# Building the kv operand of a Toeplitz convolution on VectorE in 32-bit words instead of on GpSimd

## The chip, the cores and the metric

The kernel runs on one core of a Trainium2 chip. The metric is the device time of one execution in microseconds (us); of five runs of the kernel before, the median is 862.05 us (856.38 to 877.54). All detail comes from one profiled execution of the same program.

## What is computed

Two independent heads, laid side by side in the output (2048 positions, 640 channels each):

```python
# A: gated long convolution, one filter of length S = 2048 per channel
k_shift = sum(k_pad[:, t:t + S, :] * shift_k[:, ks - 1 - t] for t in range(4))
kv = k_shift * v
y  = causal_convolution(kv, ssm_k) + kv * ssm_D      # the reference does it by FFT
a  = q * y
# B: softmax attention, 32 heads of 20 channels
q, k, v = split(x @ wqkv)
b = (softmax(q @ k.T * 20 ** -0.5) @ v) @ wo
out = concat([a, b], axis=-1)
```

All inputs and the output are bf16.

## The kernel before

**The attention sets the order of the work.** It is cut into 2,048 *units*: the scores of one head for 512 queries and 128 keys, 128 x 512 fp32, one PSUM bank each. Four units (four heads, placed in the four row strips of TensorE) share a key block. For each unit TensorE computes the scores (`S_task`, L629), an engine takes the exponential, and TensorE multiplies the probabilities with V (`PV_task`, L749), summing 16 key blocks in bank 6. Banks 0 to 2 and 3 to 5 are two halves of three units that alternate. ScalarE takes the exponential of all three units of a half in one instruction (`EXP_task`, L671, 128 x 1536), or of two (128 x 1024) while VectorE takes the third, which the text calls a *vector unit*: L691 brings it from PSUM to SBUF as 16-bit integers, and a chain of six short operations for one or two such units at a time (L721 to L731) makes the exponential by a polynomial on bit patterns. `want_vec` (L1191) decides for each half whether there is a vector unit; it asks for less than `VQ` microseconds of work queued for VectorE, and for a key block below the limits `KBV`, `KBW`.

**The convolution** is a sum of matrix products with Toeplitz blocks. A first stage (`kv_iter`, L555) makes kv on VectorE out of the shifted k, the filter taps and v (132 steps, the multiplications at L558) and writes it to a scratch tensor in DRAM in reversed order. After it, `conv_setup` (L925) starts the second stage, which runs through the rest of the kernel in 40 tasks of 16 channels. Its buffers:

- `KVr`, 128 x 64 x 80 bf16: kv of 80 channels, loaded by four DMAs (`kvr_load`, L940) every five tasks, eight times in all.
- `KVX[i]`, two buffers of 128 x 1024 bf16: for one task, kv of 16 channels, copied out of `KVr` in the order that the matmuls read. Per channel 64 columns: four groups (32-row shifts) of 16 time blocks. `kvx_build` (L950) makes it; the build of task t+2 is put in line after the last matmul of task t (L988).
- `HK`: four buffers with the Toeplitz rows of four channels each, loaded by DMA (`hk_load`).

`conv_task` (L964) issues 128 matmuls a task (L982), each with its own 128 x 128 weight load and only 26 to 32 moving columns, which it reads from `KVX` as two runs of 13 to 16 adjacent columns. They go to bank 7. Three VectorE operations (L999, L1000, L1002) bring a task's result to SBUF. `A_iter` (L1013) multiplies with q and writes the output for 160 channels at a time, 64 small steps (L1020).

In the kernel before, `kvx_build` makes two steps of 128 x 512 bf16 for GpSimd (L957): a copy whose source runs with a step of 320 elements (640 bytes) in its innermost dimension. These are GpSimd's only work in the second stage, apart from one memset (L933).

**The order on every engine is written out at build time** by a planner (L1280 to L1385). It keeps a clock for each engine, gives each operation a cost, and at each step takes for TensorE the next piece that is ready: scores, products with V, projections (L473), a few matmuls of a convolution task, or, where nothing else fits, a *filler*: a matmul of zeros (L376, `fill`, L1268) that keeps TensorE active. A filler is put in if the active time planned in the last 3.4 us is under `ZTH` and the next scores are more than `ZSL` us away (L1378); it is two matmuls if they are more than 0.45 us away. VectorE's order comes from `dve_run` (L1165): of the candidates that could start now, the one with the lowest priority number. GpSimd's came from `pool_run` (L1151). The planner holds VectorE operations that are marked as ones that share a memory port with GpSimd (`two`) back until 0.3 us before a planned GpSimd copy ends (L1133), or, if they start inside it, takes them to end 0.31 us after it (L182). Landing times of DMAs are planned as well, with 2.5 us added to the planned transfer (L193). The plan is an estimate: on the chip, engines run their lists in order and wait on semaphores.

Constants of the planner that the change touches: `KV0`, `KVPACE` (from when and at how many steps per us `kv_iter` counts as late, L1120), `APACE` (the same for `A_iter`), `VQ`, `CONVE` (how many units before the last the convolution should be done, L1204), `ZSL`, `AGE` (when an old chain of VectorE rises in priority, L1135), `LONE` (when a chain with one vector unit is closed, L1194).

Of the kernel before, what the change touches and what calls it, by code (L numbers as in the profile page):

```python
# [6 lines left out]
ALU = mybir.AluOpType  # L7
FP32 = mybir.dt.float32
BF16 = mybir.dt.bfloat16
I32, I16, U16 = mybir.dt.int32, mybir.dt.int16, mybir.dt.uint16  # L10

S = 2048
D = 640
# [16 lines left out]
NPAIR = 48  # L30
OBS = 99
NXB = 3
KBV, KBW, LONE = 13, 12, 16
CQ = 0.026
KV0, KVPACE, APACE, VQ, CONVE, ZTH, AGE, WAIT3 = 25.0, 0.8, 0.25, 4.5, 60, 2.3, 32, 0.4
TAND = 0.287
DOV, DDEP, SWITCH = 0.085, 0.03, 0.105


EXP_C = (0.07826797, 0.30457564)  # L40
DMAX = 2.0
ZSL, ZLO = 0.45, 1.8
LAT = {"pe": 0.12, "act": 0.1, "dve": 0.06, "pool": 0.1}


# [4 lines left out]
def sub(base, dims, offset=0, p0=0, pn=None):  # L50

    b = base if pn is None else base[p0:p0 + pn]
    pd = list(b.ap[0])
    return bass.AP(tensor=b.tensor, offset=b.offset + offset, ap=[pd] + [list(d) for d in dims])
# [218 lines left out]
def build_kernel(nc, A_q, A_k, A_v, A_shift_k, A_ssm_k, A_ssm_D, B_x, B_wqkv, B_wo, out):  # L273
# [3 lines left out]
    with ExitStack() as es:  # L277
        E = es.enter_context
        P = Prog(nc, E)
# [27 lines left out]
        HK_E, KVR_E, KVX_E, Y_E, AST_E = 4 * HKW, 64 * 80, 16 * 64, 16 * 160, 160  # L307
# [10 lines left out]
        def carve(n):  # L318
            a = R[:, pos[0]:pos[0] + n]
            pos[0] += n  # L320
            return a
# [6 lines left out]
        xst = [carve(4 * D).rearrange("p (t d) -> p t d", t=4) for _ in range(4)]  # L328
        pos[0] = 0
        HK = [carve(HK_E) for _ in range(NHK)]  # L330
        KVr = carve(KVR_E).rearrange("p (j c) -> p j c", j=64)
        KVX = [carve(KVX_E) for _ in range(2)]
        Y = [carve(Y_E).rearrange("p (t c) -> p t c", t=16) for _ in range(2)]
        Aq = [carve(AST_E) for _ in range(NAQ)]
# [34 lines left out]
             reads=[b_ident], writes=[b_ident])  # L369
# [26 lines left out]
        for i in range(4):  # L396
            P.dma("sp", xst[0][:, i, :], x2[i * 128:(i + 1) * 128, :], DS("x0%d" % i), writes=[b_x0[i]])
        P.op("sp", lambda e: e.dma_start(xst[1], ap(x2, [[D, 128], [128 * D, 4], [1, D]], 512 * D)),
             writes=[b_xst[1]], dsem=DS("x1"), extra=b_x0[1].w, kb=640, c=0.45)
# [13 lines left out]
        def work(prio, steps, after=None):  # L413
            if not live[0]:
                for fn, rd, wr, c, two in steps:
                    P.op("dve", fn, reads=rd, writes=wr, c=c, two=two)
                if after:
                    after()
                return None
            w = Work(prio, steps, after)  # L420
            works.append(w)
            return w
# [497 lines left out]
        cv = {}  # L920
# [19 lines left out]
        def kvr_load(b):  # L940
            P.dmas("sp", [(KVr[32 * a:32 * a + 32, 16 * a:64, :],
                           ap(kvr_d, [[D, 32], [32 * D, 64 - 16 * a], [1, 80]], 80 * b)) for a in range(4)],
                   d_kvr, reads=b_kvd, writes=[cv["KVr"]], slow=2)
# [5 lines left out]

        def kvx_build(t):  # L950
            i = t % 2
            kx = cv["KVX"][i]
            steps = []
            for z in range(2):
                dst = sub(KVX[i], [[64, 8], [16, 4], [1, 16]], 512 * z)
                src = sub(KVr, [[1, 8], [80, 4], [320, 16]], t % 5 * 16 + 8 * z)
                steps.append((lambda e, dst=dst, src=src: e.tensor_copy(dst, src), [cv["KVr"]], [kx], 1.3, False))  # L957
            pworks.append(Work(0, steps, lambda: kvr_load(t // 5 + 1) if t % 5 == 4 and t < 39 else None))

        def conv_reads(bt):  # L960
            rd = [cv["HK"][4 * bt % NHK], cv["HK"][(4 * bt + 1) % NHK], cv["KVX"][bt % 2]]
# [2 lines left out]
        def conv_task(bt):  # L964

            B, j = divmod(bt, 10)
            i = bt % 2
            for u in range(4):
                qd = bt * 4 + u
                sl = qd % NHK  # L970
                rd = [cv["HK"][sl], cv["KVX"][i]]
                for x in range(4):
                    for k in range(8):
                        d, r1 = divmod(k, 2)
                        n = 16 - d
                        last = x == 3 and k == 7
                        lhsT = HK[sl][:, x * HKW + 128 * d - 32 * r1 + 32:x * HKW + 128 * d - 32 * r1 + 160]
                        rhs = sub(KVX[i], [[32, 2], [1, n]], (4 * u + x) * 64 + r1 * 16)
                        o = sub(bank[MISC], [[256, 2], [1, n]], (4 * u + x) * 16 + d)
                        st = u + x + k == 0  # L980
                        yield (CQ, rd if x + k == 0 else [])
                        P.op("pe", lambda e, o=o, lhsT=lhsT, rhs=rhs, st=st, k=k: e.matmul(  # L982
                            o, lhsT, rhs, start=st, stop=k == 7, skip_group_check=True),
                            reads=rd, writes=[bkb[MISC]], tok=last, c=CQ, st=2 * n / 2400)
                        if last:
                            if qd + NHK < 160:
                                hk_load(qd + NHK)
                            if u == 3 and bt + 2 < 40:  # L988
                                kvx_build(bt + 2)
            M, Yb = bank[MISC], Y[B % 2]  # L990

            def after():
                conv_done[0] += 1
                if j == 9:
                    micro.append([A_iter(B), None])
                    mark[:] = [micro_n[0], P.T["pe"]]

            y, bz = cv["Y"][B % 2], cv["Z"]
            work(0.8, [(lambda e: e.tensor_copy(ZS[64:128], sub(M, [[1, 16], [16, 16]], 256, 0, 64)), [bkb[MISC]], [bz[0]], 0.425, False),  # L999
                       (lambda e: e.tensor_copy(ZS[0:64, 16:256], sub(M, [[1, 15], [16, 16]], 256, 64, 64)),  # L1000
                        [bkb[MISC]], [bz[1]], 0.41, False),
                       (lambda e: e.tensor_tensor(sub(Yb, [[160, 16], [1, 16]], 16 * j), sub(M, [[1, 16], [16, 16]]),  # L1002
                                                  ZS.rearrange("p (t x) -> p t x", t=16), ALU.add),
                        [bkb[MISC]] + bz, [y], 0.425, False)], after)

        conv_done = [0]
        pworks = []

        def A_load(B, tp):
            i = tp % NAQ  # L1010
# [137 lines left out]
                            r = max(r, busy - 0.3)  # L1148
                        yield max(T, r), 1.5 if micro_late(now) else 3, m

        def pool_run(until):  # L1151
            while P.T["pool"] <= until:
                for w in pworks:
                    st = w.steps[w.i]
                    if P.ready("pool", st[1], st[2], me=st) <= until:
                        P.op("pool", st[0], reads=st[1], writes=st[2], c=st[3], me=st)
                        w.i += 1
                        if w.i == len(w.steps):
                            pworks.remove(w)
                            w.after()  # L1160
                        break
                else:
                    return

        def dve_run(until):  # L1165
            while True:
                c = list(dve_cands(until))
# [113 lines left out]
        while nu[0] < NU or npv[0] < NB - 1 or conv_b < 40 or conv or side or pend or tail[0] < 2:  # L1281
            now = P.T["pe"]
            k = nu[0]
            bnow = k // 4
            dve_run(now)
            pool_run(now)
            P.flush(now)
            if not added and all(("X", t) in done for t in range(NKB)):
                added.append(1)
# [48 lines left out]
            if not side:  # L1338
                x = pick(bnow + 6, slack, now, bnow)
# [29 lines left out]
            if not side:  # L1369
                x = pick(NB, slack, now, bnow)  # L1370
# [9 lines left out]
            P.T["pe"] = now + 0.03  # L1380
        while micro or works or P.late:
            dve_run(P.T["pe"])
            pool_run(P.T["pe"])
            P.flush(P.T["pe"])
            P.T["pe"] += 0.1  # L1385
        live[0] = False
# [75 lines left out]
```

## Time and profile before

| | |
|---|---|
| median of five runs | 862.05 us |
| the profiled execution's own time | 864.96 us |
| its span, first to last instruction | 863.2 us |
| TensorE busy | 834.5 us, 11,659 matmuls |
| ScalarE busy | 823.7 us, 738 instructions |
| VectorE busy | 770.6 us, 1,582 instructions |
| GpSimd busy | 102.4 us, 95 instructions, 80 of them the copies of L957 |
| granted TensorE clock, mean | 0.973 of full speed |

An engine's busy time counts its instructions; waiting and issuing do not count. For TensorE it is of little use by itself, since matmuls overlap and 435 of them are fillers. A line such as "L957 POOL COPY R<-R 128x512 bf16 x80 | 90.2, 1127 | ..." reads: source line, engine (PE is TensorE, PEld its weight loads, DVE VectorE, ACT ScalarE, POOL GpSimd, SP the queue that issues most DMAs), operation, output and input tile (`R` is the memory that holds `HK`, `KVr`, `KVX`, `Y` and the probabilities), shape, count; then busy us in all and mean ns of one; then the engine's idle time just before them and what ended it.

### The profile page before, as it was taken

The page shows a single profiled execution, that of the slowest core. Times are in us where ns is not written, and L with a number is a line of the kernel's source. Part 1 is how long each engine was busy: PE and PEld are TensorE (multiplying, and loading weights), DVE is VectorE, ACT ScalarE, POOL GpSimd, SP SyncE. Part 2 cuts the span into 40 slices and gives each one's busy share as a digit, 9 for nine tenths or more (in the row PEclk, how much of TensorE's full clock was granted, in tenths as well). Part 3 has the DMA queues.
Part 4 walks back from the last instruction along what each step waited for, and adds up shares of the span by engine and source line. Part 5 has one row for each costly group of instructions (what it writes and reads, how often), then busy time and mean ns, then how long its engine had stood idle before and what let it go on. Part 6 is the DMA issues. An engine that isn't in the chain of part 4 may idle for free.

```text
span 863.2 us, 27035 instructions
## 1 busy us (share of the span) xinstructions
PE 834.5 (97%) x11659; PEld 357.6 (41%) x11659; DVE 770.6 (89%) x1582; ACT 823.7 (95%) x738; POOL 102.4 (12%) x95
## 2 busy tenths in 40 slices
PE   9999999999999999999999999999999999999998
PEld 5432332222245344454434534453443444444432
DVE  4557799998689899999999999999998999999994
ACT  6799999999789999999999999999998999999996
POOL 3000000003011121212111111211111111111100
PEclk9999999999579899999999999999998999999999
DMA  9704432219158776968876696987759469977812
GB/s 274 226 26 147 155 98 92 93 56 151 36 148 158 163 192 171 182 159 194 160 173 149 173 197 149 199 172 174 174 150 181 116 176 197 179 160 160 191 33 60
DMA packets 172994, 130.35 MB, mean 151 GB/s; under 512 B 76977, under 2 KB 170155, under 8 KB 172875
## 3 DMA queue, kind: packets, MB, share of 16 engines
q1 hardware_dynamic: 170683, 125.51, 62.7%
q0 software_dynamic: 736, 2.75, 0.9%
q8 instruction: 92, 1.51, 0.8%
q10 hardware_dynamic: 1456, 0.37, 0.2%
q14 instruction: 27, 0.22, 0.1%
HBM read 120.58 MB, written 10.61 MB: 152 GB/s over the span
## 4 chain that ended last, share of the span: by engine, by line
DVE 39%; ACT 35%; PE 24%; issue 1%; DVEq 0%
ACT R L671 35%; DVE XV L691 8%; PE PS L629 7%; PE PS L982 4%; DVE XF L728 4%; DVE XF L731 4%; PE PS L749 4%; DVE R L721 3%; PE PS L376 3%; DVE R L558 3%; PE PS L473 3%; DVE XF L726 3%; DVE XF L727 2%; DVE XF L729 2%; DVE ZS L1000 1%
## 5 line engine op out<-in xcount | busy, mean ns | idle before, releaser
L671 ACT ACTIVATE R<-PS 128x1024 bf16<-128x1024 f32 (+1 forms) x730 | 819.1, 1357 | 25.4 <-PE PS L629 25.0
L629 PE MATMUL PS<-QT,KT 20*128 20x512 bf16 x2048 | 289.1, 392 | 15.1 <-ACT R L671 5.4
L982 PE MATMUL PS<-R 128*128 128x32 bf16 (+3 forms) x5120 | 214.7, 177 | 0.5 <-DVE R L1002 0.3
L982 PEld LDWEIGHTS PS<-R 128*128 128x128 bf16 x5120 | 164.5, 96 | 105.2 <-issue 96.6
L691 DVE TENSOR_SCALAR XV<-PS 128x512 uint16<-128x512 f32 x249 | 170.0, 685 | 19.7 <-PE PS L629 18.2
L749 PE MATMUL PS<-R,V_sb 128*21 128x512 bf16 x2048 | 168.9, 393 | 3.4 <-DVE R L721 2.7
L629 PEld LDWEIGHTS PS<-QT,KT 20*128 20x128 bf16 x2048 | 71.2, 91 | 205.0 <-ACT R L671 160.8
L957 POOL COPY R<-R 128x512 bf16<-128x512 bf16 x80 | 90.2, 1127 | 514.3 <-PE PS L982 470.0
L376 PE MATMUL PS<-Zt 128*128 128x512 bf16 x435 | 141.0, 395 | 1.2 <-DVE Zt L370 1.0
L731 DVE TENSOR_TENSOR XF<-XF 128x1024 bf16<-128x1024 bf16 x125 | 89.2, 714 | 0.9
L728 DVE TENSOR_TENSOR XF<-XF 128x1024 bf16<-128x1024 bf16 x125 | 87.1, 700 | 0.4
L749 PEld LDWEIGHTS PS<-R,V_sb 128*21 128x21 bf16 x2048 | 37.4, 90 | 74.1 <-issue 44.7
L558 DVE TENSOR_TENSOR R<-R 128x640 bf16<-128x640 bf16 x128 | 61.2, 487 | 2.5
L721 DVE TENSOR_TENSOR R<-XF,XV 128x1024 uint16<-128x1024 bf16 x81 | 58.0, 717 | 0.8
L726 DVE TENSOR_SCALAR XF<-XV 128x1024 uint16<-128x1024 uint16 x125 | 53.9, 441 | 0.1
L473 PE MATMUL PS<-xT,WQ 128*20 128x512 bf16 (+1 forms) x660 | 52.0, 390 | 2.0 <-DVE XV L691 1.9
L729 DVE TENSOR_SCALAR XF<-XF 128x1024 bf16<-128x1024 uint16 x125 | 52.3, 421 | 0.5
L727 DVE TENSOR_SCALAR XF<-XF 128x1024 bf16<-128x1024 uint16 x125 | 52.2, 425 | 0.3
L376 PEld LDWEIGHTS PS<-Zt 128*128 128x128 bf16 x435 | 35.1, 99 | 37.0 <-issue 27.0
L473 PE MATMUL PS<-xT,R 128*20 128x512 bf16 (+2 forms) x660 | 45.5, 374 | 0.3 <-DVE QT L459 0.2
L723 DVE TENSOR_TENSOR R<-XF,XV 128x512 uint16<-128x512 bf16 x87 | 35.0, 429 | 0.4
L459 DVE CAST KT<-PS 128x512 bf16<-128x512 f32 (+1 forms) x32 | 21.4, 675 | 14.6 <-PE PS L473 14.5
(56 smaller groups left out, 346.0 us busy)
## 6 DMA issues: line engine op xcount, KB each, us to landing
R<-kext_scratch SPq DMA_DIRECT2D x640, 136.0 KB, 3.4
R<-in_A_k_dram SPq DMA_DIRECT2D x15, 640.0 KB, 4.0
kext_scratch<-in_A_ssm_k_dram POOLq DMA_DIRECT2D x1, 2560.0 KB, 11.5
R<-in_A_v_dram SPq DMA_DIRECT2D x16, 160.0 KB, 5.8
kvr_scratch<-R SPq DMA_DIRECT2D x16, 160.0 KB
R<-kvr_scratch SPq DMA_DIRECT2D x8, 320.0 KB, 5.7
R<-in_A_q_dram SPq DMA_DIRECT2D x64, 40.0 KB, 3.0
out_dram<-R SPq DMA_DIRECT2D x64, 40.0 KB, 3.0
```

Of the source, the lines that this page charges most:

```text
L376: P.op("pe", lambda e: e.matmul(bank[bk], Zt, zrhs, start=start, stop=start, skip_group_check=True), reads=[b_Zt], writes=[bkb[bk]], tok=s ...
L473: ins = e.matmul(bank[bk][32 * i:32 * i + DH, 0:n], Wt[:, cc, off + i * DH:off + (i + 1) * DH], xT[:, cc, x0:x0 + n], start=(cc == 0), sto ...
L558: P.op("dve", lambda e: e.tensor_tensor(o, a, b, op), reads=reads, writes=writes, c=0.486, two=True)
L629: ins = e.matmul(bank[b0 + i], KT[32 * u:32 * u + DH, g, kb * 128:(kb + 1) * 128], QT[32 * u:32 * u + DH, qs(qc, g), :], start=True, stop= ...
L671: P.op("act", lambda e: e.activation(P_sb[:, s0:s0 + m, :], PS[:, b0 * 512:(b0 + m) * 512].rearrange("p (u q) -> p u q", u=m), ACT.Exp, sc ...
L691: work(0.2, [(lambda e: e.tensor_scalar(V, bank[bk], scale * 1.4426950408889634 * 128.0, 127.0 * 128.0, op0=ALU.mult, op1=ALU.add), [bkb[b ...
L721: last = [(lambda e: e.tensor_tensor(o, Q2, V2, ALU.add), bv + [bq], [b_P[z] for z in zs], two, True)]
L728: (lambda e: e.tensor_tensor(Q, Q, F.bitcast(U16), ALU.mult), [bf, bq], [bq], two, True),
L731: (lambda e: e.tensor_tensor(Q, Q, F, ALU.mult), [bf, bq], [bq], two, True)] + last, end)
L749: ins = e.matmul(bank[OBANK][32 * u:32 * u + DH + 1, :], V_sb[:, kb, 4 * g + u, :], P_sb[:, slot[4 * b + u], :], start=first, stop=last, t ...
L957: steps.append((lambda e, dst=dst, src=src: e.tensor_copy(dst, src), [cv["KVr"]], [kx], 1.3, False))
L982: P.op("pe", lambda e, o=o, lhsT=lhsT, rhs=rhs, st=st, k=k: e.matmul(o, lhsT, rhs, start=st, stop=k == 7, skip_group_check=True), reads=rd ...
```

## The change

`kvx_build` makes one step in place of two, for VectorE in place of GpSimd: a `tensor_scalar` with a bitwise OR of zero, in unsigned 32-bit words. A word holds the bf16 values of two neighbouring channels, so 512 words are the 1,024 values of a task. Source and destination are walked as 8 channel pairs, 4 groups and 16 time blocks; the source's innermost step is 160 words, again 640 bytes. In `KVX` the two channels of a pair now lie interleaved, so `conv_task` reads its moving columns with a step of two elements; shapes, weights and the number of matmuls stay. `pool_run` and its list go. The new step takes part in VectorE's order with priority 0.8, a planned cost `KVC` = 0.45 us and the `two` mark. Eight constants of the planner take other values.

```diff
-KBV, KBW, LONE = 13, 12, 16
+KBV, KBW, LONE = 13, 12, 24
-KV0, KVPACE, APACE, VQ, CONVE, ZTH, AGE, WAIT3 = 25.0, 0.8, 0.25, 4.5, 60, 2.3, 32, 0.4
+KV0, KVPACE, APACE, VQ, CONVE, ZTH, AGE, WAIT3 = 20.0, 0.75, 0.4, 5.5, 80, 2.3, 40, 0.4
+KVC = 0.45
-ZSL, ZLO = 0.45, 1.8
+ZSL, ZLO = 0.3, 1.8
...
-        KVr = carve(KVR_E).rearrange("p (j c) -> p j c", j=64)
+        KVr2 = carve(KVR_E)
+        KVr = KVr2.rearrange("p (j c) -> p j c", j=64)
+        KVr2 = KVr2.bitcast(U32)
...
         def kvx_build(t):
             i = t % 2
-            kx = cv["KVX"][i]
-            steps = []
-            for z in range(2):
-                dst = sub(KVX[i], [[64, 8], [16, 4], [1, 16]], 512 * z)
-                src = sub(KVr, [[1, 8], [80, 4], [320, 16]], t % 5 * 16 + 8 * z)
-                steps.append((lambda e, dst=dst, src=src: e.tensor_copy(dst, src), [cv["KVr"]], [kx], 1.3, False))
-            pworks.append(Work(0, steps, lambda: kvr_load(t // 5 + 1) if t % 5 == 4 and t < 39 else None))
+            dst = sub(KVX[i].bitcast(U32), [[64, 8], [16, 4], [1, 16]])
+            src = sub(KVr2, [[1, 8], [40, 4], [160, 16]], t % 5 * 8)
+            work(0.8, [(lambda e: e.tensor_scalar(dst, src, 0, None, op0=ALU.bitwise_or), [cv["KVr"]], [cv["KVX"][i]], KVC, True)],
+                 lambda: kvr_load(t // 5 + 1) if t % 5 == 4 and t < 39 else None)
...
-                        rhs = sub(KVX[i], [[32, 2], [1, n]], (4 * u + x) * 64 + r1 * 16)
+                        rhs = sub(KVX[i], [[64, 2], [2, n]], (2 * u + x // 2) * 128 + r1 * 32 + x % 2)
...
-        pworks = []
...
-        def pool_run(until):
...
-            pool_run(now)
...
-            pool_run(P.T["pe"])
```

## The prediction

> **What bounds the kernel now.** I read the page's busy lines first, then the slices, then a table by stretch, and last the order of time around the worst stretch.
>
> ```profile
> span 863.2 us, 27035 instructions
> PE 834.5 (97%) x11659; PEld 357.6 (41%) x11659; DVE 770.6 (89%) x1582; ACT 823.7 (95%) x738; POOL 102.4 (12%) x95
> ...
> PEclk9999999999579899999999999999998999999999
> ```
>
> ScalarE is busy 95% of the span and has one kind of work, the exponentials of L671. TensorE's 97% holds 435 fillers (141.0 us) and in the list of waits its weight loads wait 160.8 us, 398 times, for ScalarE: it has room. So the span is ScalarE's work plus ScalarE's idle time, 863.2 - 823.7 = 39.5 us. The table by stretch says where it idles; its columns are PE, PEld, DVE, ACT and POOL busy with counts, granted clock, DMA share, GB/s.
>
> ```profile
> 200.00:300.00 100.00, 97.60 (x1196) 37.57 (x1194) 83.80 (x160) 87.58 (x81) 13.70 (x13) 0.81 0.65 131
> 300.00:400.00 100.00, 98.26 (x1560) 47.14 (x1560) 96.25 (x201) 99.77 (x91) 15.49 (x14) 1.00 0.77 178
> ```
>
> From 300 us on ScalarE is at 99 to 100%, but between 200 and 300 it loses 12.4 us, and there the clock is low. In rows of 5 us its busy time from 210 to 250 is 3.81, 3.91, 3.19, 4.13, 3.11, 4.19, 3.55, 3.45: 29.3 of 40, so 10.7 us lost. From 660 to 672 it is 8.42 of 12, so 3.6 us lost, at clock 0.72. The rest of the idle time is start and tail (the last exponential ends at 853.7). Order of time on VectorE, GpSimd and TensorE where the first loss begins:
>
> ```profile
> 210.38 0.89 DVE L723 TENSOR_TENSOR R<-XF,XV 128x512 uint16<-128x512 bf16 x1
> 211.20 1.32 DVE L726 TENSOR_SCALAR XF<-XV 128x1024 uint16<-128x1024 uint16 x1
> 212.56 1.20 DVE L727 TENSOR_SCALAR XF<-XF 128x1024 bf16<-128x1024 uint16 x1
> 213.68 0.68 DVE L691 TENSOR_SCALAR XV<-PS 128x512 uint16<-128x512 f32 x1
> ...
> 209.90 4.78 POOL L957 COPY R<-R 128x512 bf16<-128x512 bf16 x4 [9.83 <-DMA R<-kvr_scratch]
> ...
> 214.51 0.40 PE L629 MATMUL PS<-QT,KT 20*128 20x512 bf16 x3 [1.61 <-DVE XV L691]
> ```
>
> Four GpSimd copies run back to back from 209.9 to 214.7. In them the 0.42 us operations of VectorE take 0.89, 1.32 and 1.20 us. The evacuation behind them (L691) is late, the scores of L629 wait 1.61 us for its bank, and by the clock's records TensorE drops to half at 216.5 for 30.7 us. At half clock the scores come late for ScalarE. At 658 the same sequence stands again: two copies from 657.95, two VectorE operations of 1.32 and 1.31, a 1.0 us wait of L773 for L691, half clock from 663.7 for 6.8 us. A third drop (281.4, 6.8 us) has no such stall ahead of it.
>
> **GpSimd's copies go.** What they cost is the stretch of VectorE operations beside them; mean against median in the groups by form:
>
> ```profile
> L731 DVE TENSOR_TENSOR XF<-XF 128x1024 bf16<-128x1024 bf16 x124 | 88.8, 717 | 0.9
> L728 DVE TENSOR_TENSOR XF<-XF 128x1024 bf16<-128x1024 bf16 x124 | 86.7, 702 | 0.4
> L721 DVE TENSOR_TENSOR R<-XF,XV 128x1024 uint16<-128x1024 bf16 x81 | 58.0, 717 | 0.8
> L726 DVE TENSOR_SCALAR XF<-XV 128x1024 uint16<-128x1024 uint16 x124 | 53.6, 442 | 0.1
> ```
>
> The undisturbed (median) times are 685, 684, 684 and 420 ns, so the excess is 124 x 32 + 124 x 18 + 81 x 33 + 124 x 22 ns = 11.6 us; L727, L729, L723 and L1020 add 4.4 in the same way. All of it lies in some 28 operations that overlap a copy: **16 us of VectorE come back**. The planner holds VectorE away from planned copies, yet these collide: a copy that waits for its load starts when the load lands (209.9, 9.2 us after the first of its DMAs at 200.7), while the plan counts 1.7 + 7.4 + 2.5 = 11.6 us (L191, L193, four DMAs of 800 KB in all, counted twice).
>
> **The builds come to VectorE.** 40 operations of 512 words. The trace has no 32-bit one. Lower end: L726, whose 1,024 halfwords are as many bytes, 420 ns. Upper end, one word a cycle: L691, 512 elements in 685 ns. Between them L563 copies 640 halfwords with a step of 8 bytes in 492 ns, less than one element a cycle would give by L691's row, so a step by itself doesn't take VectorE to one a cycle. I take 420. Operations overlap by some 85 ns (684 ns ones start 600 apart), so 40 x 0.335 = 13.4 us; at 685, 24 us. **Net for VectorE: -16 + 13.4 = -2.6 us, with ends -2.6 and +8.** What it is worth: a vector unit costs VectorE (2 x 684 + 3 x 420 + 3 x 684 - 8 x 85) / 2 = 2.0 us and saves ScalarE 0.46 us (1603 - 1142 ns, forms of L671). So -2.6 us is worth -0.6 us, +8 us is +1.8.
>
> A step far beyond 8 bytes stands in no VectorE row reading SBUF. The far end is L957's own row, GpSimd with the same 640-byte step: 1,127 ns for 512 elements. The Trainium skill (SBUF — State Buffer, "Door 1: The DMA port swizzle") speaks against the change here: SBUF is read in 16-byte lines, and an access that crosses to a new line pays a penalty. By it each word of the build would pay, while moving columns 4 bytes apart, four to a line, would not. It gives no price and no row here shows the penalty on VectorE; the sum stands on the rows above.
>
> **What is queued behind a build.** VectorE runs in order; if a build waits for `kvr_load`, evacuations wait behind it and TensorE behind them. Each of the eight loads could do that once. The plan counts 11.6 us where the first load took 9.2 and single DMAs land in 3.7 to 7.9 (median 5.4), so a build is placed after its load has landed: nothing, and up to 2 us each (16 in all) if the SP queue runs late. The other builds have a task's time (copies stand 10 to 16 us apart) before they are read. SP issues the same DMAs.
>
> **Moving columns with a step of two.** 5,120 matmuls. From the starts within a run of 16 (0.55 us, the last one 0.18 long) they follow each other every 25 ns. At half clock 27 follow every 28:
>
> ```profile
> 303.84 0.55 PE L982 MATMUL PS<-R 128*128 128x32 bf16 x16
> ...
> 235.04 0.91 PE L982 MATMUL PS<-R 128*128 128x32 bf16 x27
> ```
>
> Halving the speed of the columns costs 2 to 3 ns, since the issue sets the pace. So if a step of two halved the read, the price is at most 3 x 5120 ns = 15 us of TensorE, beside 160.8 us in which it waits for ScalarE. Below nothing it can't go, as each matmul stays. I take 0 on the path; cover gone, 15 us.
>
> **The constants.** `ZSL` puts one filler into gaps of 0.3 to 0.45 us; one takes 0.215 us, which fits; it holds the clock up, and where the plan is off it delays scores by at most 0.215. `VQ`: VectorE idles 17.7 us between 300 and 800; filled, 17.7 / 2.0 x 0.46 = 4 us off ScalarE; but the builds enter the planned queue too (40 x 0.365 = 14.6 us, 7 vector units, +3.4 us). I set the two against each other: 0, ends -4 and +3.4. `KV0`, `KVPACE`: the 132 steps are due at 20 + 132 / 0.75 = 196 us in place of 190; the last ran at 192.3. `CONVE`: the same 40 tasks in some 20 units fewer, 1 to 2% denser. `APACE`, `AGE`, `LONE` change only order. Nothing for these, +-1.
>
> **Sum, against the profiled execution (864.96 us):** the stretches behind the two collisions -10.7 - 3.6, VectorE's balance -0.6: 850.1. That execution is 2.9 above the median of 862.05, so some of its loss may be less in others; I forecast a median of **850**, 1.4% below 862.
>
> The clock deserves a look: between 216.5 and 247.2 it stays at half though TensorE is busy 5.00 of each 5 us. The Trainium skill (TensorE: Matmul & The Clock Gate, "Part 1: The HAM clock gate") has the clock come back after one busy window of about 3.4 us. By that rule a drop would cost a tenth of what the trace shows, and the sum would be about 860. The measurement decides: such drops last.
>
> **The rivals.**
> 1. *Forecast, 0.58.* No collision, no stall, no drop behind it: 850, own range 844 to 857.
> 2. *The clock drops anyway where the convolution begins, 0.22.* For: the drop at 281 came without a stall; between 205 and 226 TensorE has only narrow matmuls of 20 rows or columns and fillers. Against: two of three drops follow a collision. Then only 3.6 + 0.6 is saved: 861, range 856 to 867.
> 3. *The strided build is slow and the in-order VectorE pays, 0.13; slower.* At 1.1 us (L957's row) it overruns its planned 0.45 by 0.65, 40 times: 26 us on evacuations that TensorE waits for, 850 + 26 = 876. It decides from (865 - 850) / 40 = 0.37 over the plan, a build of 0.82 us. Against: L563.
> 4. *The step of two costs several times the read, 0.05.* At 40 ns a matmul, 15 x 5120 = 77 us, half of it beside waits: about 890. Against: the half-clock row.
> 5. *The order comes out worse for some other reason, 0.02.*
>
> The change would also not do what it says if ScalarE's exponentials grew in number of units: 249 vector units now, each one fewer costs 0.46 us.
>
> **Chances.** This kernel's measurement can tell about 0.5% (4.3 us) from no change. Faster: 0.55 of case 1, 0.05 of case 2, 0.01 of others = 0.61. Same: 0.03 + 0.15 + 0.02 = 0.20. Slower 0.19. The range of 8 in 10 runs from 842 (case 1 with `VQ` filled) to 869 (cases 2 and the mild end of 3).
>
> **What would show it.** Right: the VectorE groups' means equal their medians (L731 at 685); the new build x40 at 420 with no idle before it that a DMA ended; clock near 1.0 from 205 to 300; ScalarE over 97% there; L982 25 ns apart; 245 to 255 vector units. Wrong: builds of 0.7 us or more, evacuations late behind them; `kvr_scratch` among VectorE's waits; a half-clock stretch of 30 us at the start of the convolution; fewer than 240 vector units.

## The result and the profile after

The change made no difference that shows in the comparison: the ratio to the kernel before is 0.9993, 95% interval 0.9973 to 1.0013. The median of 44 runs is 871.45 us (856.68 to 904.73), that of 79 runs of the kernel before 865.35 us (856.38 to 889.32). The ratio compares the runs with little disturbance of TensorE's clock; the medians of all runs hold that disturbance, which is a subject of its own below. The forecast was a median of 850 us, with a range of 842 to 869.

The page of the changed kernel, one execution of 880.85 us. (Lines of `kernel.py` up to 950 have moved down by three: L731 and L734 are L728 and L731 of before, L632 is L629, L674 is L671.)

```profile
span 879.1 us, 26958 instructions
PE 848.6 (97%) x11633; PEld 364.1 (41%) x11633; DVE 783.0 (89%) x1641; ACT 826.9 (94%) x744; POOL 12.2 (1%) x15
...
PEclk9999999999959999598569999999999999999999
...
L694 DVE TENSOR_SCALAR XV<-PS 128x512 uint16<-128x512 f32 x254 | 173.4, 686 | 25.8 <-PE PS L632 24.2
L379 PE MATMUL PS<-Zt 128*128 128x512 bf16 x409 | 136.6, 403 | 2.3 <-DVE OT_sb L762 1.3
L734 DVE TENSOR_TENSOR XF<-XF 128x1024 bf16<-128x1024 bf16 x128 | 87.0, 681 | 0.4
L731 DVE TENSOR_TENSOR XF<-XF 128x1024 bf16<-128x1024 bf16 x128 | 87.0, 681 | 0.2
L724 DVE TENSOR_TENSOR R<-XF,XV 128x1024 uint16<-128x1024 bf16 x87 | 59.6, 685 | 0.3
L729 DVE TENSOR_SCALAR XF<-XV 128x1024 uint16<-128x1024 uint16 x128 | 54.1, 431 | 0.1
```

GpSimd is idle but for its start and one memset, the stretched operations are gone (L734 has a mean of 681 and L724 of 685 where the kernel before had 717 and 717; one operation of L729 alone was stretched, beside the memset), vector units went from 249 to 254, fillers from 435 to 409. But VectorE's busy time is not lower (783.0 us against 770.6), and ahead of the tail the clock falls to half four times, for 95.6 us together, where the kernel before had three such drops of 44.3 us. The new line by itself (durations are min, median, max in ns) and the table by stretch:

```profile
L957 DVE TENSOR_SCALAR R<-R x40: 596/607/636, 221.6 to 822.2; 128x512 uint32<-128x512 uint32 x40
its engine sat idle before it (us, times) until:
  PE PS L982: 0.2, 1
```

```profile
300.00:400.00 100.00, 97.41 (x1429) 42.95 (x1426) 90.78 (x187) 92.00 (x82) 0.00 (x0) 0.86 0.71 160
400.00:500.00 100.00, 97.96 (x1305) 41.53 (x1305) 85.98 (x178) 87.23 (x80) 0.00 (x0) 0.78 0.64 137
...
600.00:700.00 100.00, 96.78 (x1534) 47.34 (x1526) 97.06 (x199) 99.29 (x90) 0.00 (x0) 1.00 0.76 167
```

The build takes 607 ns (median), not 420. No DMA ends a wait ahead of it. And ScalarE (fourth number after the width) is at 98 to 99% where the clock is 1.00, at 92 and 87% where it is 0.86 and 0.78: the loss that the kernel before has between 210 and 250 us stands here between 241 and 453.

### The profile page after: what moved, and what is told of

Read it like the earlier page. It is cut to its first block, busy times and chain, and to the rows that moved or that the text cites. A ratio compares the mean times of both kernels' runs of the same rounds, so it can differ in the third digit from the quotient of the medians.

```text
span 879.1 us, 26958 instructions
## 1 busy us (share of the span) xinstructions
PE 848.6 (97%) x11633; PEld 364.1 (41%) x11633; DVE 783.0 (89%) x1641; ACT 826.9 (94%) x744; POOL 12.2 (1%) x15
## 4 chain that ended last, share of the span: by engine, by line
DVE 44%; PE 29%; ACT 23%; issue 2%; DMA 1%; SPq 0%; DVEq 0%
ACT R L674 23%; DVE XV L694 10%; PE PS L632 9%; PE PS L982 6%; PE PS L752 5%; DVE XF L734 5%; DVE XF L731 4%; PE PS L379 4%; DVE R L724 3%; DVE XF L729 3%; DVE XF L732 3%; DVE XF L730 2%; PE PS L476 2%; DVE R L726 2%; DVE R L957 2%
## 5 line engine op out<-in xcount | busy, mean ns | idle before, releaser
L674 ACT ACTIVATE R<-PS 128x1024 bf16<-128x1024 f32 (+1 forms) x736 | 822.4, 1293 | 38.0 <-PE PS L632 36.4
L632 PE MATMUL PS<-QT,KT 20*128 20x512 bf16 x2048 | 298.7, 402 | 13.7 <-ACT R L674 4.6
L982 PE MATMUL PS<-R 128*128 128x32 bf16 (+3 forms) x5120 | 217.3, 178 | 1.7 <-DVE R L1002 1.3
L982 PEld LDWEIGHTS PS<-R 128*128 128x128 bf16 x5120 | 167.9, 97 | 122.1 <-issue 113.3
L694 DVE TENSOR_SCALAR XV<-PS 128x512 uint16<-128x512 f32 x254 | 173.4, 686 | 25.8 <-PE PS L632 24.2
L752 PE MATMUL PS<-R,V_sb 128*21 128x512 bf16 x2048 | 174.9, 401 | 4.9 <-DVE R L726 1.9
L632 PEld LDWEIGHTS PS<-QT,KT 20*128 20x128 bf16 x2048 | 72.3, 91 | 189.0 <-ACT R L674 140.0
L379 PE MATMUL PS<-Zt 128*128 128x512 bf16 x409 | 136.6, 403 | 2.3 <-DVE OT_sb L762 1.3
L734 DVE TENSOR_TENSOR XF<-XF 128x1024 bf16<-128x1024 bf16 x128 | 87.0, 681 | 0.4
L731 DVE TENSOR_TENSOR XF<-XF 128x1024 bf16<-128x1024 bf16 x128 | 87.0, 681 | 0.2
L724 DVE TENSOR_TENSOR R<-XF,XV 128x1024 uint16<-128x1024 bf16 x87 | 59.6, 685 | 0.3
L729 DVE TENSOR_SCALAR XF<-XV 128x1024 uint16<-128x1024 uint16 x128 | 54.1, 431 | 0.1
L534 PE MATMUL PS<-R,xT 128*128 128x160 bf16 (+1 forms) x240 | 30.8, 257 | 0.8 <-DVE KT L462 0.4
L726 DVE TENSOR_TENSOR R<-XF,XV 128x512 uint16<-128x512 bf16 x80 | 31.0, 419 | 0.1
```

The lines of the kernel that those rows point to most:

```text
L379: P.op("pe", lambda e: e.matmul(bank[bk], Zt, zrhs, start=start, stop=start, skip_group_check=True), reads=[b_Zt], writes=[bkb[bk]], tok=s ...
L632: ins = e.matmul(bank[b0 + i], KT[32 * u:32 * u + DH, g, kb * 128:(kb + 1) * 128], QT[32 * u:32 * u + DH, qs(qc, g), :], start=True, stop= ...
L674: P.op("act", lambda e: e.activation(P_sb[:, s0:s0 + m, :], PS[:, b0 * 512:(b0 + m) * 512].rearrange("p (u q) -> p u q", u=m), ACT.Exp, sc ...
L694: work(0.2, [(lambda e: e.tensor_scalar(V, bank[bk], scale * 1.4426950408889634 * 128.0, 127.0 * 128.0, op0=ALU.mult, op1=ALU.add), [bkb[b ...
L724: last = [(lambda e: e.tensor_tensor(o, Q2, V2, ALU.add), bv + [bq], [b_P[z] for z in zs], two, True)]
L729: (lambda e: e.tensor_scalar(F.bitcast(U16), V, 127, None, op0=ALU.bitwise_and), bv, [bf], one, True),
```

## Two numbers for a kernel, not one

Every run lists its mean granted clock. In the clock records of all profiles but that of e5 it takes two values only, full and half; a change from full to half is called a *drop* here. Over the 44 runs of the changed kernel, time is a straight line in it: 848.3 + 589 x (1 - clock), with a residual of 0.8 us and a correlation of -0.998. A clock of 0.9 means 0.1 x 2 of the span at half clock, so **each us at half clock goes with 0.34 us of time** (589 over twice the mean span of 870 us). The time of a kernel is then told by two numbers that can be compared one by one: its time at a given clock (0.975 is taken, where most runs lie), and how long it runs at half clock. The lines of the other kernels of the table have the same slope within 10%. The last column is the ratio as above, to runs of the kernel before made beside those of the row.

| kernel | runs | time at clock 0.975 | mean time at half clock | ratio, 95% interval |
|---|---|---|---|---|
| before (beside the experiments) | 102 | 864.6 +-0.2 | 45 +-2 | 1 |
| changed | 44 | 863.0 +-0.3 | 71 +-5 | 0.9993 (0.9973-1.0013) |
| e1 before, two builds | 11 | 856.7 +-0.5 | 51 +-7 | 0.9929 (0.9887-0.9972) |
| e2 changed, two builds | 12 | 856.9 +-0.9 | 97 +-11 | 0.9973 (0.991-1.0036) |
| e3 changed, old constants | 12 | 862.4 +-0.7 | 67 +-13 | 0.999 (0.9935-1.0045) |
| e4 before, new constants | 12 | 868.5 +-0.5 | 49 +-10 | 1.0069 (1.0008-1.0129) |
| e6 changed, step of one | 12 | 862.9 +-0.8 | 70 +-9 | 1.0015 (0.9958-1.0072) |
| e7 changed, adjacent source | 12 | 858.0 +-0.8 | 72 +-7 | 1.0009 (0.9962-1.0056) |
| e9 before, step of two | 12 | 865.3 +-0.7 | 54 +-9 | 0.9956 (0.9896-1.0017) |
| e8 changed, planned 0.61 | 12 | 859.3 +-0.4 | 51 +-8 | 0.9914 (0.9866-0.9962) |
| r1 as e3, planned 0.61 | 6 | 861.3 +-0.6 | 48 +-14 | 0.9893 (0.9844-0.9942) |
| r2 changed, VQ 5.4 | 12 | 864.6 +-0.4 | 43 +-6 | 0.9984 (0.994-1.0029) |
| r3 as e8, VQ 5.4 | 7 | 859.0 +-1.0 | 28 +-7 | 0.9884 (0.9838-0.993) |
| r4 before, VQ 4.4 | 12 | 864.2 +-0.9 | 87 +-14 | 1.0088 (1.0051-1.0124) |

The +- of the third column is twice the standard error of the fitted line, that of the fourth one standard error. Of the kernel before, two of 104 runs, with a clock under 0.8, are left out; on four chips it stood at 40 to 51 us of half clock, and in 11 further runs beside r5, on one of these chips, at 30 +-5. So the second number has 10 to 20 us in it that don't come from the kernel; single runs of one kernel scatter by 17 to 49 us (standard deviation). One run of e1, of 1,229 us at full clock, is left out too.

## The experiments

**Where do drops come from?** For each of the profiled executions I laid windows of 3.41 us on the moments at which the clock changed (they are whole multiples of it apart) and added up the time in which TensorE's columns moved, with what overlaps counted once, at 2.4 columns a ns (two fillers of 512 columns start 0.215 us apart where they follow most closely). The median window at full clock has a share of 0.64. Fifteen profiles (all but those of e5, e11, e12 and r5) have 49 drops before 830 us; the window ahead of each has a share of 0.25 to 0.57, 44 or more of the 49 under 0.54. (A share is good to some 0.05: it depends on whether the columns are placed at the start or at the end of a matmul's record.) Not every such window brings a drop: of some 3,300 windows at full clock that bring none, 105 to 160 are under 0.54, in the changed kernel some of 0.49 and 0.50. So a thin window stands ahead of every drop, and about one thin window in four brings one. That was theory B, against theory A of the prediction, that collisions make the drops.

### e1 and e2: hardly any builds

```diff
         def kvx_build(t):
             i = t % 2
+            if t >= 2:
+                if t % 5 == 4 and t < 39:
+                    kvr_load(t // 5 + 1)
+                return
```

> The kernel before, with GpSimd's copies made for tasks 0 and 1 alone (the later 38 tasks read the kv of those two, so their output is not the convolution's). Theory A (collisions): without copies there are no stretched VectorE operations, no stalls behind them and no half clock behind those; clock 0.985 or more, time near 850. Theory B (active share): every drop of the clock in the two profiles follows a window of 3.41 us in which TensorE's columns moved for under about half of it (0.36 to 0.52), and the plan runs near that share everywhere; then the half-clock time stays (clock 0.96 to 0.98), and fast runs stand at 857 to 862, the 16 us of VectorE being worth at most 3 us.

> The changed kernel with the builds on VectorE made for tasks 0 and 1 alone (later tasks read the kv of those two). It takes 38 x 0.607 us of VectorE away. If the builds are what ate the gain (theory C: 20 us of VectorE and evacuations late behind them), time falls to near 850 and the clock rises above 0.985. Theory B: within 0.5% of the changed kernel's fast runs (858 to 863), half-clock stretches as before.

Measured: 857.9 and 874.2 us in the median, and 856.7 and 856.9 at clock 0.975. So the builds cost 7.9 us on GpSimd (864.6 - 856.7) and 6.1 us on VectorE (863.0 - 856.9), at a given clock. That is about twice what the prediction's exchange rate gives for VectorE's time (16 and 13.4 us of it: 3.7 and 3.1 us), and far from 14 us.

The half-clock time did not go: 51 us in e1 as in its kernel before, and 97 in e2, the most of the twelve-run kernels, although it has two builds in all. Theory C fails as an explanation of the half-clock time. For theory A e2 and the changed kernel are what counts: they have no GpSimd copy at all, and 97 and 71 us of half clock. e1 can't decide it, since it keeps the four copies at 210 us, and its profile has the drop that follows them, at 215.8, behind a window under 0.3.

In all four profiles with GpSimd's copies and the old constants, up to small edits (before, e1, e9, r4), the clock drops at 215.8 to 216.5, behind a TensorE wait of 1.1 to 1.7 us for L691 and a window of 0.25 to 0.36, and stays at half for 27 to 31 us: 119 of the 239 us at half clock that the four have before 830 us. No profile without the copies has a drop there (that of e5, at a clock of 0.85 nearly throughout, apart); the first comes at 233.7 us or later, with the old constants (e3) at 468.6. And e4 has the copies without the stall. They run from 216.3 to 221.6 us, two operations of VectorE are stretched, but TensorE's matmuls wait 0.5 us at most for L691 (below the order of time, then the waits from 205 to 222 us: us in all, times, longest):

```profile
216.31 5.28 POOL L957 COPY R<-R 128x512 bf16<-128x512 bf16 x4 [10.39 <-DMA R<-kvr_scratch]
216.68 1.30 DVE L727 TENSOR_SCALAR XF<-XF 128x1024 bf16<-128x1024 uint16 x1
219.11 1.56 DVE L728 TENSOR_TENSOR XF<-XF 128x1024 bf16<-128x1024 bf16 x1
```

```profile
PE PS L629 <- DVE XV L691: 0.7, 2, 0.5
```

Its first drop is at 318.7. So that step of the prediction, collision, stall, drop, stands for this place, and without the copies the drop there is gone, as forecast. What doesn't follow is that the half-clock time goes with it: e4 lacks this drop and has 49 us of half clock in the mean, e3 67, e2 97.

### e3 and e4: the move alone, the constants alone

```diff
 (e3, the changed kernel)
-KBV, KBW, LONE = 13, 12, 24
+KBV, KBW, LONE = 13, 12, 16
-KV0, KVPACE, APACE, VQ, CONVE, ZTH, AGE, WAIT3 = 20.0, 0.75, 0.4, 5.5, 80, 2.3, 40, 0.4
+KV0, KVPACE, APACE, VQ, CONVE, ZTH, AGE, WAIT3 = 25.0, 0.8, 0.25, 4.5, 60, 2.3, 32, 0.4
-ZSL, ZLO = 0.3, 1.8
+ZSL, ZLO = 0.45, 1.8
 (e4: the same lines the other way, in the kernel before)
```

> The changed kernel with the constants of the kernel before (the builds stay on VectorE, moving columns with a step of two): the move alone. Theory A: 850. Theory B: 860 to 864 in fast runs, clock as in the kernel before (0.97). If the constants D (fewer fillers, 409 against 435, a denser convolution) brought more half clock, this one has less of it than the changed kernel.

> The kernel before with the changed kernel's constants: the constants alone. Theory A: collisions stay, so 862 to 866. Theory D: more half-clock time than in the kernel before, all runs' median some 5 us above it, fast runs equal.

Measured at clock 0.975: e3 862.4, e4 868.5. The move alone saves 2.2 us, the constants alone cost 3.9 us beside GpSimd's copies and 0.6 us (within the error) beside VectorE's builds. Half clock 67 and 49: theory D, that the constants bring it, falls with both (the changed kernel has 71, the kernel before 51 in its runs beside these).

### e6 and e9: the step of the moving columns

```diff
 (e6, the changed kernel)
-rhs = sub(KVX[i], [[64, 2], [2, n]], (2 * u + x // 2) * 128 + r1 * 32 + x % 2)
+rhs = sub(KVX[i], [[64, 2], [1, n]], (2 * u + x // 2) * 128 + r1 * 32 + 16 * (x % 2))
 (e9: the changed kernel's line in the kernel before)
```

> The changed kernel, same order on every engine, with moving columns read as 13 to 16 adjacent elements (from a place in KVX that holds other values, so the sums are not the convolution's). Kernels with a step of two spent 67 to 97 us at half clock, those without 49 to 51 (means). Theory E (the step of two makes TensorE count as less active): half-clock time falls to about 50, median to 865. Theory F (the order with the builds does it): it stays near 71, median 871. Both: the time at a given clock doesn't move by over 1 us, as matmuls follow each other every 25 ns with either step.

> The kernel before, same order, with the changed kernel's way of reading moving columns (a step of two, other values). Theory E: half-clock time rises from 51 to about 70 us, median from 866 to 872. Theory F: both stay. Both: time at a given clock within 1 us.

Measured: 862.9 against 863.0, and 865.3 against 864.6 at clock 0.975; half clock 70 +-9 against 71, and 54 +-9 against 44 +-5 beside it. The matmuls' rows in e6 and in the changed kernel (min, median, max ns):

```profile
L982 PE MATMUL PS<-R x5120: 174/176/234, 222.9 to 837.2; 128*128 128x32 bf16 x50, 128*128 128x30 bf16 x49, 128*128 128x28 bf16 x49, 128*128 128x26 bf16 x49
```

```profile
L982 PE MATMUL PS<-R x5120: 175/176/234, 222.9 to 846.0; 128*128 128x32 bf16 x50, 128*128 128x30 bf16 x49, 128*128 128x28 bf16 x49, 128*128 128x26 bf16 x49
```

176 ns with either step, and 25 ns from start to start in both. The step of two costs nothing that shows; theory E falls.

### e7 and e10: why a build takes 607 ns

```diff
 (e7)
-src = sub(KVr2, [[1, 8], [40, 4], [160, 16]], t % 5 * 8)
+src = sub(KVr2, [[64, 8], [16, 4], [1, 16]], t % 5 * 512)
 (e10)
-dst = sub(KVX[i].bitcast(U32), [[64, 8], [16, 4], [1, 16]])
-src = sub(KVr2, [[1, 8], [40, 4], [160, 16]], t % 5 * 8)
+dst = sub(KVX[i].bitcast(U32), [[1, 16], [16, 4], [64, 8]])
+src = sub(KVr2, [[160, 16], [40, 4], [1, 8]], t % 5 * 8)
```

> The changed kernel, same order, with the build's source read as adjacent words in place of a step of 160 words (so KVX holds other values). It measures what the 640-byte step costs on VectorE: 420 ns in place of 607 if the step does it, 607 still if 32-bit words do. 40 x 0.187 = 7.5 us of VectorE at 420: at a given clock 0 to 2 us faster, since nothing else is moved.

> The changed kernel with the build's loops turned round: the eight channel pairs, adjacent words in the source, run innermost, and the destination takes the step (64 words). The output is the full one, and so is the order on every engine. If only reads pay for a step: 420 ns and the time of adjacent words, 858 at clock 0.975. If writes pay as much: 607 and 863.

The build's row in e7 and in e10:

```profile
L957 DVE TENSOR_SCALAR R<-R x40: 416/420/429, 221.0 to 807.7; 128x512 uint32<-128x512 uint32 x40
```

```profile
L957 DVE TENSOR_SCALAR R<-R x40: 590/605/628, 221.6 to 816.6; 128x512 uint32<-128x512 uint32 x40
```

With adjacent words on both sides it takes 420 ns, as the prediction had it; a step of 640 bytes on the read costs 187 ns, a step of 256 bytes on the write 185. Turning the loops round gains nothing (e10: 860.6 +-2.2 at clock 0.975 from six runs of nearly one clock, too wide to tell; half clock 86). At a given clock e7 is 5.0 us faster than the changed kernel in the same order: 40 x 0.187 = 7.5 us of VectorE were worth 5.0 us, 0.67 us for each, not the 0.23 of the prediction's exchange rate (0.46 / 2.0).

### e8: the plan is told the truth

```diff
-KVC = 0.45
+KVC = 0.61
```

> The changed kernel with the build's planned cost KVC at its measured 0.61 us in place of 0.45. Theory G (the plan is short by 0.157 us x 40 = 6 us, and evacuations come late behind it): the time at a given clock falls by 2 to 5 us towards that of adjacent words (858 at clock 0.975, against 863). Theory H (VectorE's time itself is what costs: 7.5 us more of it a run): it stays within 1 us of 863, since the planner only gives away three vector units for it. The half-clock time may move either way, as the order is another one.

Measured: 859.3 at clock 0.975, 3.7 us less than the changed kernel, with the builds at 608 ns; median 863.3 of 12 runs, ratio 0.9914. Its tables of waits add up to 10.2 us of TensorE behind VectorE (29 waits), where the changed kernel has 16.5 us (46) and e7 7.7 us (24). (With `VQ` at 5.4, in r2 and r3 below, the same sums are 13.7 and 11.1 us: the same direction, but less than the time that is saved.) A place where it is seen in the changed kernel, VectorE and then TensorE:

```profile
406.11 0.61 DVE L957 TENSOR_SCALAR R<-R 128x512 uint32<-128x512 uint32 x1
406.75 0.42 DVE L999 COPY ZS<-PS 64x256 f32<-64x256 f32 x1
407.20 0.41 DVE L1000 COPY ZS<-PS 64x240 f32<-64x240 f32 x1
407.65 0.69 DVE L762 CAST OT_sb<-PS 128x512 bf16<-128x512 f32 x1
```

```profile
407.09 0.39 PE L632 MATMUL PS<-QT,KT 20*128 20x512 bf16 x3
408.39 0.40 PE L752 MATMUL PS<-R,V_sb 128*21 128x512 bf16 x4 [0.91 <-DVE OT_sb L762]
```

A build stands ahead of the evacuation of bank 6 (L762), TensorE waits 0.91 us for that bank, and the clock is halved from 408.8 for 44 us. Theory G at this point; but another planned cost is another order too, so it could have been chance (theory L).

### r1 to r4: is it the plan, or the draw?

```diff
 (r1) e3 with KVC = 0.61
 (r2) the changed kernel, (r3) e8:
-... VQ, ... = 20.0, 0.75, 0.4, 5.5, 80, 2.3, 40, 0.4
+... VQ, ... = 20.0, 0.75, 0.4, 5.4, 80, 2.3, 40, 0.4
 (r4) the kernel before: VQ 4.5 to 4.4
```

> The changed kernel with the old constants and the true planned cost of the build. The same with KVC at 0.45 stood at 862.4 at clock 0.975 and 67 us of half clock (mean). Theory G: it falls by 3 to 4 us to 859, half clock to about 50. Theory L: within 859 to 866 either way, half clock anything from 45 to 100.

> The changed kernel with VQ at 5.4 in place of 5.5: another order, nothing else. Theory G: 863 at clock 0.975 within 1 us, half clock near 71. Theory L: it differs from the changed kernel as much as the true planned cost does (3.7 us, 20 us of half clock).

> The changed kernel with the true planned cost and VQ at 5.4. Theory G: 859 at clock 0.975 within 1 us, as with VQ at 5.5, and half clock near 51. Theory L: anything in 856 to 866.

> The kernel before with VQ at 4.4 in place of 4.5: another order. Theory G: 864.5 at clock 0.975 within 1 us, half clock 40 to 51. Theory L: differs by 3 us or more, and half clock may be 70.

At clock 0.975: r2 864.6 (changed 863.0), r3 859.0 (e8 859.3), r4 864.2 (before 864.6), r1 861.3 (e3 862.4). A change of order that means nothing moves this number by 0.3 to 1.6 us in the three pairs tried; the true planned cost moves it by -3.7 and -5.6 with the new constants, by -1.1 +-0.9 with the old ones. So theory G holds for the new constants, in both pairs, and is open for the old ones. Half clock is another matter: 71 against 43, 51 against 28, 45 against 87 (one run of 199 us in it; 77 without) between orders that differ by 0.1 in `VQ`. The first two pairs were measured at different hours, which can make 10 to 20 us; r4's 87 stands against 42 of the kernel before beside it. Of the four kernels with one and the same order, changed, e6 and e7 stand at 70 to 72, e10 at 86 +-6. **The mean half-clock time goes with the order that happened to be planned** (theory L), and no effect of the builds on it shows.

### e5, e12 and r5: can fillers hold the clock?

```diff
-ZSL, ZLO = 0.3, 1.8
+ZSL, ZLO = 0.3, 2.2        (e5)      1.9 (e12 and r5)
-... CONVE ... 80           (r5, with KVC = 0.61)
+... CONVE ... 160
```

> The changed kernel with ZLO at 2.2 in place of 1.8: convolution steps get a filler ahead of them more often, so fewer windows are active for under half. In the runs so far time is a straight line in the clock: 848 us at full clock plus 0.34 us for each us at half clock (44 runs of the changed kernel). Theory B: half-clock time falls from 71 us (mean) to under 20; if the fillers fit into TensorE's waits the median falls to 850 to 856. If TensorE has no room for them, the full-clock time rises by 10 us or more and nothing is gained.

> The changed kernel with ZLO at 1.9 in place of 1.8, some 90 fillers more (2.2 gave 785 more, a clock of 0.99 in its undisturbed runs, and a convolution that came 170 us late). Theory B: half-clock time falls from 71 to 30 to 50 us and the median to 858 to 864; the time at full clock rises by 0 to 5 us.

> The changed kernel with the true planned cost (0.61), ZLO at 1.9 and CONVE at 160 (the convolution is due 80 units, some 34 us, earlier). Theory B: clock 0.985 or more in nearly all runs (half clock under 25 us) and, as the convolution's late end is gone, 846 to 852 in the median with little spread. If the activity of a window isn't the cause, half clock stays at 30 to 70 us; if the fillers themselves are what cost, the clock is 0.99 and the time above 855.

Medians 1029.9, 877.5 and 881.7 us, ratios 1.195, 1.017 and 1.028: all slower. Yet the clock did what theory B says: 0.995 or 0.996 in four of r5's six runs and 0.988 in the others, 12 +-3 us of half clock against 51 in e8, which has the same planned cost, and 30 in the kernel before beside r5. e12 has 34 +-14. r5 by stretch:

```profile
300.00:400.00 100.00, 98.32 (x1510) 44.99 (x1507) 98.53 (x203) 99.87 (x93) 0.00 (x0) 1.00 0.68 155
...
840.00:879.00 39.00, 25.68 (x307) 14.11 (x308) 10.79 (x31) 1.08 (x2) 0.00 (x0) 0.89 0.55 115
```

Until 800 us ScalarE is at 99.5% and more, and at the end it waits 42.4 us for TensorE (L905 behind L864 in its waits). What is left then is the convolution (the last L982 at 854.2) and the output of A. The same step is at 815.4 in e8. A filler goes ahead of a convolution step in the same gap, so 120 fillers more (547 against e8's 425) mean fewer steps, and an earlier due time doesn't help a convolution that is short of gaps: that is my reading of the planner. That the activity of a window makes the drops rests on two things, the thin window ahead of all 49 and the clock of r5 and e12; this way of adding activity costs more than it saves.

### e11: no build at all

```diff
-rhs = sub(KVX[i], [[64, 2], [2, n]], (2 * u + x // 2) * 128 + r1 * 32 + x % 2)
+rhs = sub(KVr, [[160, 2], [320, n]], bt % 5 * 16 + 4 * u + x + 80 * r1)
 (and kvr_load after the last matmul of every fifth task)
```

> No build at all: the matmuls read their moving columns from KVr with a step of 320 elements (640 bytes), and a load of KVr waits for the last matmul of five tasks, so the convolution pauses some 12 us eight times. The output is the full one. If a moving column with that step is read as fast, matmuls stay 25 ns apart and the time at clock 0.975 is that of the kernel with two builds, 857. If the step slows the read as it does VectorE (607 to 420), 26 to 32 columns take 16 to 19 ns and are still under the 25 ns of the issue. Only a read over twice as slow shows: at 40 ns, 77 us of TensorE and 890 or more.

Measured: 1,235 us. Its matmuls, in the same columns as above:

```profile
L980 PE MATMUL PS<-R x5120: 204/229/246, 221.4 to 1200.5; 128*128 128x32 bf16 x50, 128*128 128x30 bf16 x49, 128*128 128x28 bf16 x49, 128*128 128x26 bf16 x49
```

From start to start they stand 48 ns apart with 26 columns and 58 with 32, some 1.8 ns a column, and the same at full and at half clock. Adding 27 ns to 5,120 matmuls gives 138 us of the 363 that e11 takes over the changed kernel. The rest falls in a run whose mean clock is 0.672 and in which the convolution pauses for eight loads; the two weren't taken apart. That slow columns leave TensorE inactive and so bring the half clock fits theory B, but is argued. The build earns its time.

## Why the prediction was wrong

**The step that failed** is the first term of the sum, "the stretches behind the two collisions -10.7 - 3.6": the half-clock time behind the collisions was taken off as if nothing else would bring such time. The drop behind the first collision did go (e3, the changed kernel), but drops at other places came in its stead: 71 us of half clock in the mean where the kernel before has 45, +9 us in place of -14.3. What the runs show, step by step:

1. *ScalarE's work plus its idle time makes the span*: right. In the stretches of 100 us at full clock after 300 us it is at 98 to 100% in every profile read so (before, changed, e8, r3, r4, r5), and the idle time goes with the clock (0.34 us for 1 us at half clock). The price that the prediction took, 14.3 us for 37.5 us at half clock, was about right too.
2. *Collision, stall, drop*: right at 216 us in four profiles, and e4, with the copies but without the stall, has no drop there. But it was one place out of many. The plan runs at a share of 0.64 in the median window and comes under 0.54 again and again, since convolution matmuls follow each other every 25 ns and, at 2.4 columns a ns, move their 26 to 32 columns in only 11 to 13 of them. A different order has its thin windows elsewhere: half clock is 71 us in the changed kernel, 43 in the same kernel with `VQ` at 5.4, and 45 in the kernel before. Rival 2 ("the clock drops anyway", 861, at 0.22) came nearest, but it put the drop where the convolution begins. The changed kernel has none from 205 to 226 us; its four come at 241 to 409. That the clock can drop without a collision at any thin place was seen in the drop at 281 and given no term in the sum.
3. *The Trainium skill's rule on the clock* (TensorE: Matmul & The Clock Gate, "Part 1: The HAM clock gate", one busy window of about 3.4 us brings the clock back) doesn't describe these drops: in the changed kernel they last 23.9, 3.4, 23.9 and 44.4 us with TensorE busy for 95.6 of these 95.6 us in the profile. That part of the prediction, that the measurement decides and such drops last, held.
4. *16 us of VectorE come back*: right in size (L734 and L731 have a mean of 681 at a median of 684), too low in price. A vector unit's exchange rate (0.46 us for 2.0) makes 3.7 us of it. e1 shows the copies' whole price, 7.9 us at a given clock, of which nine more vector units (258 against 249) are 4.1; the rest wasn't taken apart.
5. *Builds of 420 ns*: mis-sized, 607. I leaned on L563, whose step of 8 bytes costs nothing to speak of, against the Trainium skill, which speaks of a penalty for an access that crosses to a new 16-byte line (SBUF — State Buffer, "Door 1: The DMA port swizzle"). Here the runs agree with it: 0.37 ns a word for a step of 640 bytes on the read (607 against 420 ns) and of 256 bytes on the write (605). 40 builds take 40 x (0.607 - 0.085) = 20.9 us in place of 13.4, and the 7.5 us more are worth 5.0 us (e7); telling the plan the true 0.61 gets 3.7 us back with the build as slow as before (e8). Rival 3 had this mechanism: by its reckoning a build 0.157 us over the plan costs 40 x 0.157 = 6.3 us, where 3.7 to 5.0 were measured.
6. *No wait for loads ahead of a build*: right, 0.2 us in 40 builds, and TensorE ended it.
7. *The step of two costs nothing*: right (e6, e9), within 0.1 and 0.7 us, less than the error of each.
8. *The constants cost nothing*: right beside VectorE's builds (+0.6, within the error), wrong beside GpSimd's copies (+3.9, e4). 254 vector units lie within the 245 to 255 named.

**The sum as it came out, at clock 0.975.** The kernel with its builds all but gone stands at 857 with either engine (e1, e2). GpSimd's copies add 7.9 us, VectorE's builds 6.1: the change saves 1.6 +-0.4 us, where e8's true planned cost saves 5.3. On top comes the half-clock time, 26 us more in this order than in the kernel before, times 0.34: 9 us. Together +7, as the means differ by 6.9 (872.1 to 865.2, the latter beside the experiments); in the result's own runs the means differ by 4.6 (872.1 to 867.5) and the medians by 6.1. The ratio of the result, 0.9993, shows no difference.

What stays open: why a particular window under 0.54 brings a drop and another doesn't, and why a drop lasts 3.4 us at one place and 44 at another. The same order doesn't drop at the same places every time: e10, with the changed kernel's order and builds as long as its, has its first drop at 340.5 us, not at 241.5. At half clock, counted at 1.2 columns a ns (fillers then start 0.40 to 0.43 us apart), the window ahead of a return holds 0.75 or more, but so do most that bring no return. With the old constants the true planned cost may be worth nothing (r1, -1.1 +-0.9). That a build put ahead of an evacuation costs by making TensorE wait is shown at one place and by sums of waits of one execution each; the price at a given clock (e8, r3) is measured.

**Two versions are ahead of both kernels at a given clock**: e8 (ratio 0.9914, 0.9866 to 0.9962) and r3 (0.9884, 0.9838 to 0.993; median 851.1), which differ from the changed kernel only in the planned cost of the build, and r3 in `VQ`. r1 (0.9893) has as low a ratio in six runs. At a given clock e8 gains 5.3 us and r3 5.6. e8's median, 863.3, is no lower than the 862.3 of the kernel before beside it, which had 40 us of half clock to e8's 51; r3's is 10.6 lower, and what goes beyond 5.6 is its 28 us at half clock, a fortunate order that was measured in seven runs.

## What to carry to other kernels

Where the clock of TensorE comes and goes, compare kernels by the time at a given clock and by the time at half clock; a stall that is removed at one place is worth its own length, and the drop behind it only if the new order has no thin window elsewhere. When work is moved to an engine whose order is planned ahead, measure it and give the planner the measured cost first: here 0.16 us on 40 operations decided between 863 and 859 at a given clock. A strided operation is priced by a row with the same step, not by one with a short step.

## What the runs showed of the hardware

- VectorE, 512 words of 32 bits from SBUF to SBUF: 420 ns with adjacent words, 607 with a source step of 640 bytes, 605 with a destination step of 256 bytes.
- TensorE reads moving bf16 columns with a step of 4 bytes as fast as adjacent ones (25 ns a matmul of 26 to 32 columns); with 640 bytes a column takes some 1.8 ns, at either clock (48 ns for 26, 58 for 32).
- TensorE's clock: every one of 49 drops to half stands behind a window of 3.41 us in which columns moved for 0.25 to 0.57 of the time (median window 0.64), and lasts 3.4 to 61 us; each us at half clock goes with 0.34 us of this kernel's time.
- Fillers on a larger scale (1,194 of them, e5) left five of six runs at a clock of 0.99 or more; the profiled execution had 0.85 nearly from start to end.
